# An attention and MoE kernel on one core: the second group's q on ScalarE's queue, the third pair's v on GpSimd

## The chip, the core and the metric

The kernel runs on one NeuronCore of one Trainium2 chip. The metric is the device time of one execution in microseconds; before the change it is 595.95 us, the median of 3 runs (595.73 to 596.18).

## What is computed

Attention over q, k and v of shape (2, 12, 448, 64), and behind it two feed-forward layers over 896 tokens (768 to 2048 to 768, twice). The two matrices of a layer come as 64-bit floats.

```python
scores = cap * np.tanh(scale * q @ k.T / cap)
attn = np.exp(scores - max); attn = attn / (attn.sum(-1) + 1e-09)
x = (attn @ v) as (batch * seq, heads * head_dim)
h = x @ w_in;  x = where(h > 0, h, exp(min(h, 0)) - 1) @ w_out
h = x @ w_in2; out = relu(h) ** 2 @ w_out2
```

## The kernel before, in words

**Pairs and groups.** The 24 heads are worked on as 12 pairs, n = 0 to 11; two pairs are a group (L77). Of a group's q, k and v the first 384 rows of each head are loaded into one tile each (`nat[g]`, three transfers each, one for every 128 rows, L117 and L132); the last 64 rows go to tiles of their own: `qz` (one transfer, L122), `kz` (two, L127) and `vs` (two, L139). `load_group` (L103) issues them, on SP's queue unless another is named. Group 0 is loaded in two halves, one for each pair, so its transfers are half as large.

**One pair.** TensorE transposes ten 128-column blocks, k with its tail and q with its tail, into PSUM tile `pt` (`turn`, L170). ScalarE casts the whole to tf32-like `kqh` (`high`, L182), VectorE subtracts to get the rest `kql` (`low`, L188). TensorE makes the scores in four chunks c (`scores`, L224), each of which takes one of two PSUM tiles `sc`; ScalarE applies tanh to each chunk (`tanh`, L240) and exp to the first two and to the last two chunks (`exp`, L250). VectorE splits the result into `ph` and `pl` (`split_p`, L254). v is split into `vh` and `vl` by `prep_v` (L144): `vl` on GpSimd for every pair, `vh` on GpSimd for pairs 0 and 1 and on VectorE from pair 2 on (L153). TensorE multiplies v and p in two parts (`pv`, L266), ScalarE copies the result out (`pv_out`, L292), and VectorE scales it by the sums a few pairs later (`norm`, `norm_x`).

**Order.** The whole stands under `tc.manual_schedule()` (L535): every engine and queue keeps the order of the program text. The opening (L536 to L558) issues loads, makes the first pair in `first_pair` (L198: TensorE transposes pair 0, with products of the identity to fill its time; ScalarE makes three casts at L220; VectorE three subtractions), then `scores(0, 0)`, `scores(0, 1)` and `turn(1)`. The loop at L574 runs over the pairs. In iteration 0 the order on ScalarE is tanh(0,0), tanh(0,1), high(1), exp(0,0), tanh(0,2), tanh(0,3), exp(0,1), then tanh(1,0) and high(2); on TensorE it is scores(0,2), scores(0,3), nine identity products (L594, eighteen records in the profile), scores(1,0), scores(1,1), turn(2), pv(0,0), then scores(1,2). On VectorE, `prep_v(2)` stands in iteration 1 ahead of `low(2)` and of the split of pair 1.

**Transfers and their completion counters.** The framework lays the instructions of all engines in one list, by its own estimate of when each starts, and numbers the transfers of both queues along that list. Eight completion counters serve them in turn, so the issue of every transfer waits until the transfer eight numbers before it, of either queue, has landed. A DMA issue stands in the order of the engine that makes it: one that waits on ScalarE holds what ScalarE has behind it. In the program before, the list runs so around the change; the first pair's third cast on ScalarE stands between numbers 32 and 33. At the list's beginning, where both queues issue, their transfers alternate one by one: 1, 3, 5, 7, 9 and 11 are ScalarE's (q with its tail of pair 0, cap, a piece of w_in), 2, 4, 6, 8, 10 and 12 are SP's.

```
12-16 k, kz of pair 1 (SP)       17-20 q, qz of pair 1 (SP)
21-25 v, vs of pair 0 (SP)       26-28 k of group 1 (SP)
29-30 kz of group 1 (SP)         31-33 q of group 1 (SP)
34    qz of group 1 (SP)         35-39 v, vs of pair 1 (SP)
40    w_in piece (SP)            41-45 v, vs of group 1 (SP)
```

After attention come the two feed-forward layers. Their matrices are streamed in pieces, and VectorE and ScalarE turn each piece into a high and a low part.

Of the kernel before, what the change touches and what calls it, by code (L numbers as in the profile page):

```python
# [26 lines left out]
def attention_moe_kernel(  # L27
# [12 lines left out]
    nc = tc.nc  # L40
    B, H, S, D = q.shape
# [46 lines left out]
    qzs = [one.tile([P, 4, D], F32, name=f"qz{i}") for i in range(2)]  # L88
# [4 lines left out]
    def fill_kq(i, eng):  # L93
        eng.memset(kzs[i], 0.0)
        eng.memset(qzs[i][D:], 0.0)
# [4 lines left out]
        if i < 2:  # L100
            eng.memset(vss[i][:, :, D:], 1.0)

    def load_group(g, what="kqvw", pp=None, dma=nc.sync.dma_start):  # L103

        if 2 * g >= len(pairs):
            return
        b, hp = pairs[2 * g]
        h0, nh = (0, 4) if pp is None else (2 * pp, 2)
        hs = slice(2 * hp + h0, 2 * hp + h0 + nh)
        if g not in nat:  # L110
            nat[g] = {x: lp.tile([P, NFULL, 4, D], F32, name=x, tag=x) for x in "kqv"}
        tail = slice(NFULL * P, S)
        for x, src in (("k", k), ("q", q)):
            if x in what:
                t = nat[g][x][:, :, h0:h0 + nh]
                src = src[b, hs]
                for c in range(NFULL):  # L117
                    dma(  # L118
                        t[:, c], src[:, c * P:(c + 1) * P].rearrange("h p d -> p h d")
                    )  # L120
                if x == "q":
                    dma(  # L122
                        qzs[g % 2][:D, h0:h0 + nh], src[:, tail].rearrange("h p d -> p h d")
                    )
                else:
                    for hh, r in enumerate(ROWS):
                        dma(  # L127
                            kzs[g % 2][r, h0 // 2:(h0 + nh) // 2, r],
                            src[hh::2, tail].rearrange("h p d -> p h d"),
                        )  # L130
        if "v" in what:
            for c in range(NFULL):  # L132
                dma(
                    nat[g]["v"][:, c, h0:h0 + nh],
                    v[b, hs, c * P:(c + 1) * P].rearrange("h p d -> p h d"),
                )
        if "w" in what:
            for hh, r in enumerate(ROWS):
                dma(  # L139
                    vss[g % 2][r, h0 // 2:(h0 + nh) // 2, :D],  # L140
                    v[b, hs][hh::2, tail].rearrange("h p d -> p h d"),
                )

    def prep_v(n):  # L144
        if n >= len(pairs):
            return
        g, pp = divmod(n, 2)
        vh, vl = vhs[n % 3], vls[n % 3]
        vn = nat[g]["v"][:, :, 2 * pp:2 * pp + 2]
        h, l = (t.rearrange("p (c h) d -> p c h d", h=2)[:, :, :, :D] for t in (vh, vl))  # L150


        (nc.vector if n > 1 else nc.gpsimd).tensor_copy(h, vn)  # L153
        nc.gpsimd.tensor_tensor(l, vn, h.bitcast(F32), op=ALU.subtract)


# [2 lines left out]
    def turn_one(to, n, u, c):  # L159
        g, pp = divmod(n, 2)  # L160
        hs = slice(2 * pp, 2 * pp + 2)
        if c < NFULL:
            src = nat[g]["kq"[u]][:, c, hs].rearrange("p h d -> p (h d)")
        elif u == 0:
            src = kzs[g % 2][:, pp]
        else:
            src = qzs[g % 2][:, hs].rearrange("p h d -> p (h d)")
        nc.tensor.transpose(to, src, ident)  # L168
# [13 lines left out]
    def high(n):  # L182
        if n >= len(pairs):
            return
        st["qk", n] = [ap_.tile([P, 2, W], F32R, name=x, tag=x) for x in ("kqh", "kql")]
        nc.scalar.copy(used(st["qk", n][0]), used(st["pt", n]))

    def low(n):  # L188
        if n >= len(pairs):
            return  # L190
        h, l, t = (used(x) for x in (*st["qk", n], st["pt", n]))
        nc.vector.tensor_tensor(l, t, h.bitcast(F32), op=ALU.subtract)

    def idle_products(to, n):
        for _ in range(n):
            nc.tensor.matmul(to[:, 0, :P], ident, ident, start=True, stop=True)

    def first_pair():  # L198

        idle = psc.tile([P, 2, W], F32, name="sc", tag="sc")
        warm = lambda n: idle_products(idle, n)
        qk = [ap_.tile([P, 2, W], F32R, name=x, tag=x) for x in ("kqh", "kql")]
        st["qk", 0] = qk
        warm(8)
        pieces = []
        for u, cs, pool, tag, after in (
            (0, range(NFULL), ps1, "pt", 2),
            (1, range(NFULL + 1), ps1, "po", 0),  # L210
            (0, range(NFULL, NFULL + 1), psc, "sc", 6),
        ):
            t = pool.tile([P, 2, W], F32, name=tag, tag=tag)
            at = slice(cs[0] * P, (cs[-1] + 1) * P)
            for c in cs:
                turn_one(t[:, u, c * P:(c + 1) * P], 0, u, c)
            warm(after)
            pieces.append((t[:, u, at], *(x[:, u, at] for x in qk)))
        for t, h, l in pieces:
            nc.scalar.copy(h, t)  # L220
        for t, h, l in pieces:
            nc.vector.tensor_tensor(l, t, h.bitcast(F32), op=ALU.subtract)
# [17 lines left out]
    def tanh(n, c):  # L240
        if c == 0:
            st["e", n] = ap_.tile([P, NB, S], F32, name="e", tag="e")
        w = 2 if c < NFULL else 1
        nc.scalar.activation(  # L244
            st["e", n][:, 2 * c:2 * c + w], st["sc", n, c][:, :w, :S], AF.Tanh, scale=tsc
        )
# [3 lines left out]
    def exp(n, i):  # L250
        e = st["e", n][:, PARTS[i]]
        nc.scalar.activation(e, e, AF.Exp, scale=capt)  # L252

    def split_p(n, i, copy=nc.vector.tensor_copy):  # L254
        if n < 0:
            return
        if i == 0:
            st["p", n] = [
                ap_.tile([P, NB - 1, S], F32R, name=x, tag=x, bufs=1) for x in ("ph", "pl")
            ]  # L260
        blocks = slice(PARTS[i].start, min(PARTS[i].stop, NB - 1))
        e, h, l = (t[:, blocks] for t in [st["e", n]] + st["p", n])
        copy(h, e)
        nc.vector.tensor_tensor(l, e, h.bitcast(F32), op=ALU.subtract)
# [270 lines left out]
    with tc.manual_schedule():  # L535
        fill_kq(0, nc.vector)  # L536
        load_group(0, "k", 0)
        load_group(0, "q", 0, dma=nc.scalar.dma_start)
        nc.scalar.dma_start(capt, cap.unsqueeze(0).to_broadcast([P, 1]))
        ws.load(nc.scalar.dma_start)  # L540
        load_group(0, "kq", 1)
        load_group(0, "vw", 0)
        fill_kq(1, nc.gpsimd)
        load_group(1, "kq")
        load_group(0, "vw", 1)
        ws.load()
        load_group(1, "vw")
# [2 lines left out]
        fill_v(2, nc.gpsimd)  # L550
        np_ = len(pairs)
        first_pair()
        nc.vector.reciprocal(tsc, capt)
        nc.vector.tensor_scalar(tsc, tsc, 1.0 / math.sqrt(D), None, op0=ALU.mult)
        prep_v(0)
# [18 lines left out]
        for n in range(np_):  # L574
            last = n == np_ - 1
            tanh(n, 0)
            if n:
                high(n + 1)
            tanh(n, 1)
            if not n:  # L580
                high(n + 1)
            split_p(n - 1, 1)
            prep_v(n + 1)
            exp(n, 0)
            low(n + 1)
            if n == 2:
                emit(second[3:])
            scores(n, 2)
            pv(n - 1, 1)
            scores(n, 3)  # L590
            if n:
                turn(n + 2)
            else:
                idle_products(ps1.tile([P, 2, W], F32, name="po", tag="po"), 9)  # L594
            norm(n - 2)
            if last:
                emit(ws.start())
            tanh(n, 2)
            pv_out(n - 1)
            if 2 <= n < 7:  # L600
                ws.load()
            tanh(n, 3)
            exp(n, 1)
            emit(norm_x(n - 3))
            split_p(n, 0)
            if n == 1:
                second = ws.whole()
                emit(second[:3])
            scores(n + 1, 0)
            scores(n + 1, 1)  # L610
            if not n:
                turn(2)
            if last:

                begun.append(new_acc())
                mm_in(0, 0, begun[0], xh, xl, kb[0:6:2])
            pv(n, 0)

            if n % 2:
                load_group((n + 3) // 2, "qv" if n > 1 else "v")  # L620
            else:
                load_group(n // 2 + 2, "k" if n else "kq")
                load_group(n // 2 + 1, "w" if n else "")


# [12 lines left out]
        x, x_high, x_low = norm_x(np_ - 2)  # L638
# [9 lines left out]
        x, x_high, x_low = norm_x(np_ - 1, nc.scalar.copy)  # L648
# [166 lines left out]
```

## Time and profile before

| | |
|---|---|
| median of 3 runs | 595.95 us (595.73 to 596.18) |
| the profiled execution | 594.1 us, of which 592.3 us from the first to the last instruction |
| busy | TensorE 98%, its weight loads 89%, VectorE 72%, ScalarE 56%, GpSimd 5% of the span |
| mean granted TensorE clock | 0.997 of 2.4 GHz |
| 40 slices of 14.8 us | TensorE at 9 tenths or more in all but the first and the last; the granted clock is below 9 tenths in one slice, the second |

The profiled execution is 1.85 us under the median. Times in the profile count from the start of the span. PE is TensorE, PEld its weight loads, DVE VectorE, ACT ScalarE, POOL GpSimd; SPq and ACTq are the queues on which SP and ScalarE issue transfers. A row of a timeline gives start, duration, engine, line, operation, what it writes and reads, how many instructions are merged, and in brackets the idle time before it with what ended it. A row of a table by windows gives for each stretch its length, the busy time of each engine, TensorE's granted clock, the DMA engines' busy share and GB/s.

### The profile page before, as it was taken

To read this page: it belongs to the slowest core of one execution; us is meant where nothing else is said; L and a number is where in the kernel's file an instruction comes from. 1 tells how busy PE (TensorE), PEld (TensorE's weight loads), DVE (VectorE), ACT (ScalarE), POOL (GpSimd) and SP (SyncE) were. 2 spreads that over 40 slices of the span, in tenths; PEclk is the share of its full clock that TensorE was granted. 3 is DMA by queue.
4 is the path that set the end of the run, shared out by engine and by line. 5 is a ranking of instruction groups with operands and counts; after the bars stand their busy time and mean duration, and the time that the engine had idled before them with its cause. 6 is when DMAs were issued, how large, how long until landed. Compare 5 with 4: busy or idle time off the path is not lost.

```text
span 592.3 us, 8596 instructions
## 1 busy us (share of the span) xinstructions
PE 583.4 (98%) x3062; PEld 528.0 (89%) x3062; DVE 425.0 (72%) x845; ACT 334.2 (56%) x484; POOL 32.1 (5%) x46
## 2 busy tenths in 40 slices
PE   8899999999999999999999999999999999999997
PEld 8677777788999999999999999999999999999997
DVE  4599999989999888665666657777777599981000
ACT  5699999827898777433333335666666645441000
POOL 3110110000000000000000000000000011230000
PEclk9899999999999999999999999999999999999999
DMA  5645651024444333233333344333333346622000
GB/s 128 158 103 140 161 148 42 33 75 144 135 133 134 106 98 100 76 128 106 116 98 107 111 132 132 107 107 107 108 114 113 108 136 184 184 70 106 24 23 37
DMA packets 81980, 64.76 MB, mean 109 GB/s; under 512 B 38416, under 2 KB 77072, under 8 KB 81936
## 3 DMA queue, kind: packets, MB, share of 16 engines
q1 hardware_dynamic: 80432, 63.58, 36.8%
q10 hardware_dynamic: 1504, 0.62, 0.4%
q8 instruction: 24, 0.39, 0.3%
q14 instruction: 20, 0.16, 0.1%
HBM read 61.34 MB, written 2.80 MB: 108 GB/s over the span
## 4 chain that ended last, share of the span: by engine, by line
PE 90%; DMA 3%; DVE 3%; SPq 2%; ACT 1%; issue 1%; POOL 0%; ACTq 0%; POOLq 0%; DVEq 0%
PE acc L522 19%; PE acc L523 19%; PE acc L521 19%; PE po L287 8%; PE acc L746 7%; PE acc L745 7%; PE acc L747 7%; PE sc L235 4%; PE pt L168 1%; DMA q<-in_q_dram 1%; SPq L118 1%; DVE xn L327 1%; DMA far<-rd 1%; DMA bc<-far 1%; DMA qz<-in_q_dram 0%
## 5 line engine op out<-in xcount | busy, mean ns | idle before, releaser
L521 PE MATMUL acc<-xh,wh 128*128 128x448 f32 x384 | 139.8, 364 | 1.2 <-ACT xh L333 1.2
L522 PE MATMUL acc<-xl,wh 128*128 128x448 f32 x384 | 140.0, 365 | 0.2 <-DVE xl L334 0.2
L523 PE MATMUL acc<-xh,wl 128*128 128x448 f32 x384 | 139.9, 364 | 0.0
L446 ACT CAST wh<-wf 128x384 fp32r<-128x384 f32 (+2 forms) x114 | 57.9, 508 | 107.2 <-PE acc L522 87.5
L391 ACT ACTIVATE wf<-wst 128x384 f32<-128x384 f32 (+2 forms) x130 | 70.5, 543 | 60.5 <-DVE wl L441 33.7
L441 DVE TENSOR_TENSOR wl<-wf,wh 128x384 fp32r<-128x384 f32 (+2 forms) x116 | 63.6, 548 | 55.9 <-ACT wh L446 55.8
L521 PEld LDWEIGHTS acc<-xh,wh 128*128 128x128 f32 x384 | 72.1, 188 | 7.1 <-ACT xh L333 1.5
L522 PEld LDWEIGHTS acc<-xl,wh 128*128 128x128 f32 x384 | 72.1, 188 | 5.9 <-DVE xl L334 0.5
L523 PEld LDWEIGHTS acc<-xh,wl 128*128 128x128 f32 x384 | 72.1, 188 | 5.7 <-DVE wl L441 0.3
L432 DVE SCALAR_TENSOR_TENSOR wf<-wst,wf 128x384 uint32<-128x384 uint32 (+3 forms) x132 | 71.1, 539 | 0.1
L425 DVE SCALAR_TENSOR_TENSOR wf<-wst,wf 128x384 uint32<-128x384 uint32 (+3 forms) x132 | 70.9, 537 | 0.0
L522 PE MATMUL acc<-gl,wh 128*128 128x448 f32 x192 | 70.0, 365 | 0.0
L523 PE MATMUL acc<-gh,wl 128*128 128x448 f32 x192 | 70.0, 364 | 0.0
L521 PE MATMUL acc<-gh,wh 128*128 128x448 f32 x192 | 69.8, 364 | 0.0
L404 DVE TENSOR_SCALAR wf<-wf 128x384 uint32<-128x384 uint32 (+3 forms) x132 | 54.4, 412 | 0.7
L400 DVE TENSOR_SCALAR wf<-wf 128x384 f32<-128x384 f32 (+3 forms) x132 | 45.7, 346 | 7.5 <-ACT wf L391 7.5
L244 ACT ACTIVATE e<-sc,tsc 128x896 f32<-128x896 f32 (+1 forms) x48 | 43.4, 911 | 2.9 <-PE sc L235 2.9
L732 DVE COPY o<-acc 128x432 f32<-128x432 f32 (+1 forms) x8 | 4.5, 557 | 53.8 <-PE acc L747 45.7
L746 PE MATMUL acc<-wl,gh 128*128 128x432 f32 x112 | 40.3, 359 | 0.0
L745 PE MATMUL acc<-wh,gh 128*128 128x432 f32 x112 | 40.0, 357 | 0.0
L747 PE MATMUL acc<-wh,gl 128*128 128x432 f32 x112 | 39.9, 356 | 0.0
L252 ACT ACTIVATE e<-e,capt 128x1792 f32<-128x1792 f32 (+1 forms) x24 | 38.6, 1609 | 0.8
(94 smaller groups left out, 933.0 us busy)
## 6 DMA issues: line engine op xcount, KB each, us to landing
wst<-in_moe_w_in_dram SPq DMA_DIRECT2D x63, 384.0 KB, 3.2
wst<-in_moe_w_out_dram SPq DMA_DIRECT2D x24, 384.0 KB, 3.2
wst<-in_moe_w_out_dram SPq DMA_DIRECT2D x16, 432.0 KB, 3.2
wst<-in_moe_w_out_dram SPq DMA_DIRECT2D x16, 336.0 KB, 2.9
wst<-in_moe_w_out_dram SPq DMA_DIRECT2D x12, 256.0 KB, 2.7
bc<-far SPq DMA_DIRECT2D x12, 224.0 KB, 3.3
k<-in_k_dram SPq DMA_DIRECT2D x15, 128.0 KB, 3.7
q<-in_q_dram SPq DMA_DIRECT2D x15, 128.0 KB, 2.9
```

The source lines that it names most:

```text
L391: nc.scalar.activation(self.f[i], hi.bitcast(F32), AF.Abs)
L404: v.tensor_scalar(fb, fb, 3, 0x3FFFFFFF, op0=ALU.logical_shift_left, op1=ALU.bitwise_and)
L425: v.scalar_tensor_tensor(out=fb, in0=hi, scalar=0xC0000000, in1=fb, op0=ALU.bitwise_and, op1=ALU.bitwise_or,)
L432: v.scalar_tensor_tensor(out=fb, in0=lo, scalar=29, in1=fb, op0=ALU.logical_shift_right, op1=ALU.bitwise_or,)
L441: (v if dst is None else nc.gpsimd).tensor_tensor(wl, self.f[i], wh.bitcast(F32), op=ALU.subtract)
L446: (v.tensor_copy if self.alone else nc.scalar.copy)(wh, self.f[i])
L521: nc.tensor.matmul(acc, w[0], x[0], start=first, stop=False)
L522: nc.tensor.matmul(acc, w[0], x[1], start=False, stop=False)
L523: nc.tensor.matmul(acc, w[1], x[0], start=False, stop=last)
L745: nc.tensor.matmul(acc, gh[:, f, gs], w[0], start=a, stop=False)
L746: nc.tensor.matmul(acc, gh[:, f, gs], w[1], start=False, stop=False)
L747: nc.tensor.matmul(acc, gl[:, f, gs], w[0], start=False, stop=z)
```

## The change

`load_group` gets a letter of its own, "z", for the tail of q; where q was loaded, its tail still is, right behind it, with one exception. For group 1, the three large q transfers are no longer issued by SP between kz and qz; ScalarE issues them after `first_pair`, that is behind its three casts and ahead of tanh(0,0). The tail qz of group 1 stays on SP, right behind kz. And `prep_v` makes `vh` of pair 2 on GpSimd instead of VectorE.

```diff
-    def load_group(g, what="kqvw", pp=None, dma=nc.sync.dma_start):
+    def load_group(g, what="kqzvw", pp=None, dma=nc.sync.dma_start):
...
         for x, src in (("k", k), ("q", q)):
+            src = src[b, hs]
             if x in what:
                 t = nat[g][x][:, :, h0:h0 + nh]
-                src = src[b, hs]
                 for c in range(NFULL):
                     dma(
                         t[:, c], src[:, c * P:(c + 1) * P].rearrange("h p d -> p h d")
                     )
-                if x == "q":
-                    dma(
-                        qzs[g % 2][:D, h0:h0 + nh], src[:, tail].rearrange("h p d -> p h d")
-                    )
-                else:
+                if x == "k":
...
+        if "z" in what:
+            dma(qzs[g % 2][:D, h0:h0 + nh], q[b, hs, tail].rearrange("h p d -> p h d"))
...
-        (nc.vector if n > 1 else nc.gpsimd).tensor_copy(h, vn)
+        (nc.vector if n > 2 else nc.gpsimd).tensor_copy(h, vn)
...
-        load_group(0, "q", 0, dma=nc.scalar.dma_start)
+        load_group(0, "qz", 0, dma=nc.scalar.dma_start)
...
-        load_group(0, "kq", 1)
+        load_group(0, "kqz", 1)
...
-        load_group(1, "kq")
+        load_group(1, "kz")
...
         first_pair()
+        load_group(1, "q", dma=nc.scalar.dma_start)
         nc.vector.reciprocal(tsc, capt)
...
-                load_group((n + 3) // 2, "qv" if n > 1 else "v")
+                load_group((n + 3) // 2, "qzv" if n > 1 else "v")
             else:
-                load_group(n // 2 + 2, "k" if n else "kq")
+                load_group(n // 2 + 2, "k" if n else "kqz")
```

## Rows read from the trace of the kernel before

**Rows 1.** The chain that ended last, 0 to 70 us: start, us, what.
```profile
1.79 2.72 DMA q<-in_q_dram
...
4.53 0.37 SPq L118
...
20.17 4.06 PE po L287 x12
...
27.81 0.96 PE pt L168 x8
...
30.18 2.67 PE po L287 x12
...
38.73 2.71 PE po L287 x12
```
**Rows 2.** TensorE's timeline, 10 to 24 us.
```profile
11.20 0.47 PE L235 MATMUL sc<-kqh 64*128 64x448 f32 x2
...
16.49 0.55 PE L168 MATMUL pt<-ident,k 128*128 128x128 f32 x3
...
19.87 0.30 PE L168 MATMUL pt<-ident,qz 128*128 128x128 f32 x1 [0.22 <-DMA qz<-in_q_dram]
```
**Rows 3.** Table by windows, 17 to 24 us.
```profile
17.00:20.00 3.00, 1.45 (x7) 0.71 (x6) 1.93 (x3) 0.89 (x1) 0.00 (x0) 1.00 0.78 175
20.00:23.00 3.00, 3.00 (x9) 2.66 (x9) 0.00 (x0) 2.76 (x3) 1.42 (x2) 0.52 0.44 115
23.00:24.00 1.00, 1.00 (x5) 0.77 (x3) 0.00 (x0) 0.90 (x1) 0.09 (x1) 0.74 1.08 297
```
**Rows 4.** ScalarE's timeline, 5 to 24 us.
```profile
7.68 0.27 ACT L220 CAST kqh<-sc 128x128 fp32r<-128x128 f32 x1
9.67 1.91 ACT L244 ACTIVATE e<-sc,tsc 128x896 f32<-128x896 f32 x2 [1.72 <-PE sc L235]
...
16.90 0.99 ACT L244 ACTIVATE e<-sc,tsc 128x896 f32<-128x896 f32 x1
20.21 0.96 ACT L186 CAST kqh<-pt 128x960 fp32r<-128x960 f32 x1 [2.32 <-PE pt L168]
```
**Rows 5.** VectorE's timeline, 26 to 28 us.
```profile
26.01 0.55 DVE L153 CAST vh<-v 128x384 fp32r<-128x384 f32 x1 [7.04 <-DMA v<-in_v_dram]
26.48 1.15 DVE L192 TENSOR_TENSOR kql<-pt,kqh 128x960 fp32r<-128x960 f32 x1
```
**Rows 6.** Issues on SP's and ScalarE's queues, 0 to 20 us (timeline).
```profile
0.73 1.55 ACTq L118 DMA_DIRECT2D q<-in_q_dram  x3
...
11.81 1.69 SPq L118 DMA_DIRECT2D k<-in_k_dram  x3
13.61 1.67 SPq L127 DMA_DIRECT2D kz<-in_k_dram  x2
15.32 1.69 SPq L118 DMA_DIRECT2D q<-in_q_dram  x3
17.06 0.61 SPq L122 DMA_DIRECT2D qz<-in_q_dram  x1
```
**Rows 7.** What SP's queue waited for, 0 to 140 us: us in total, times, longest.
```profile
SPq L118 <- DMA q<-in_q_dram: 0.4, 1, 0.4
```
**Rows 8.** Transfers issued from 10.6 to 15.3 us: count, KB each, median us to landing.
```profile
vs<-in_v_dram SPq DMA_DIRECT2D x2, 16.0 KB, 2.0
...
k<-in_k_dram SPq DMA_DIRECT2D x3, 128.0 KB, 3.7
...
kz<-in_k_dram SPq DMA_DIRECT2D x2, 32.0 KB, 3.0
```
**Rows 9.** GpSimd's timeline, 21 to 22 us.
```profile
21.50 0.50 POOL L153 CAST vh<-v 128x384 fp32r<-128x384 f32 x1 [7.32 <-DMA v<-in_v_dram]
```
**Rows 10.** TensorE's timeline, 109 to 119 us.
```profile
109.66 1.08 PE L287 MATMUL po<-pl,vh 128*128 128x448 f32 x4 [0.24 <-DVE pl L264]
...
118.26 1.08 PE L287 MATMUL po<-pl,vh 128*128 128x448 f32 x4 [0.19 <-DVE pl L264]
```

## The prediction

> **What bounds the kernel now.** I read the page first, then the chain that ended last in its first 70 us, then TensorE, ScalarE, VectorE and both issuing queues there. From about 30 us on TensorE is without a gap: the twelve products of pv start 8.55 us apart (30.18, then 38.73) [rows 1]. In the pair before, the same step took 10.01 us (20.17 to 30.18) [rows 1]: its first twelve products lasted 4.06 instead of 2.67 us. The table by windows shows why: from 17 to 20 us TensorE was busy for 1.45 of 3 us, and from 20 us on its granted clock was 0.52, then 0.74, of full speed [rows 3], that is at the lower level of 1.2 GHz for most of that time. It was idle for group 1's q: turn(2) begins at 16.49, but its last block, qz, runs at 19.87 [rows 2]. ScalarE's high(2) waits 2.32 us for that block and starts at 20.21 [rows 4]. So whatever moves high(2) and pv(0,0) moves all that follows; the change aims at this place. Both come at the end of a ScalarE queue that runs without a gap from tanh(0,0) at 9.67 to tanh(1,0) at 16.90 [rows 4].
>
> **The wait that comes with an issue.** A transfer's issue waits until the transfer eight numbers before it has landed, on either queue. The trace shows this across the queues: SP's second k transfer of pair 1 (number 13) is asked for at 4.53, and what the chain has ahead of it is the landing of ScalarE's third q transfer (number 5), 1.79 to 4.51 [rows 1]; SP's queue has that as a wait of 0.4 us [rows 7]. So a ScalarE issue can be held by an SP transfer.
>
> The Trainium skill ("DMA: Bandwidth & Descriptors", the section on the anatomy of one DMA) says that DMA engines don't wait on semaphores: the wait happens on the issuing sequencer, ahead of dispatch. The trace agrees, as far as that 0.4 us of SP's queue goes; of a held ScalarE it shows nothing.
>
> **The change part by part.**
>
> *The three q issues on ScalarE.* By themselves they are free: three took 1.55 us on ScalarE's queue at the start [rows 6], and between the third cast's end at 7.95 and tanh(0,0) at 9.67 ScalarE waits 1.72 us for scores [rows 4]. Their numbers are not free. The list has the third cast between numbers 32 and 33. Without q, SP's qz becomes 31 and the first v transfer of pair 1 becomes 32, so ScalarE's first is 33 or 34. At the list's beginning the two queues alternate one by one; I let them do so here, which makes the three 33, 35 and 37. They wait for 25 (the second vs transfer of pair 0), 27 (the second k of group 1) and 29 (the first kz of group 1). All three are issued by SP later than 7.95, and SP has nothing that lets it come there sooner. The third decides: kz is issued at 13.61 [rows 6] and takes 3.0 us to land [rows 8], 16.6. With 0.52 us for the issue itself (a third of 1.55) ScalarE is free at about 17.1. Tanh(0,0) waits behind, ready since 9.67: held by about **7.5 us**.
>
> *Who waits for tanh(0,0).* Two scores tiles are filled, so scores(0,2), at 11.20 before [rows 2], must wait until tanh(0,0) has read the first. One tanh is 0.96 us (half of 1.91) [rows 4]: scores(0,2) starts at about 18.15. From there to turn(2) TensorE had 5.29 us (11.20 to 16.49) [rows 2], of which 0.17 was a wait; I take 5.1, and 0.96 for the eight transposes of a turn [rows 1]. TensorE has then stood idle for some 6.9 us. Already 1.55 us of idleness in 3 us was followed by the lower level [rows 3], so I add one such stretch at the price that it has there: 3 x 0.48 + 0.26 = 1.7 us. turn(2) ends at 18.15 + 5.1 + 0.96 + 1.7 = 25.9. On ScalarE, tanh(1,0) comes at 16.90 + 7.5 = 24.4 and is out by 25.4, so TensorE is the later of the two. q itself, asked for by 17.1 and 3.7 us on its way at most (k's time) [rows 8], is in by 20.8 and late for nobody.
>
> *What comes back.* pv(0,0) now runs at full speed, since the slow stretch lies earlier: 8.55 us to the next pv instead of 10.01. pv(1,0) starts at 25.9 + 8.55 = 34.45 instead of 30.18: **+4.3 us**. TensorE has no gap later in which to catch up.
>
> *SP's queue.* It loses three issues, so qz goes at 15.32 instead of 17.06 [rows 6], and all of v, vs and the w_in piece behind it are 1.74 us earlier. Each is needed only after high(2) and pv(0,0), which are now later: nothing gained. The eighth transfers behind ScalarE's three (41, 43 and 45, group 1's v and vs) are asked for at about 20 us and wait for nothing that lands after 20.8; at worst some 1 us, with nobody waiting.
>
> *vh of pair 2.* On VectorE it waited 7.04 us for v and held low(2), which came at 26.48 [rows 5]. Now GpSimd makes it; a cast there takes 0.50 us [rows 9] against 0.55 on VectorE, and GpSimd is idle for 7.32 us before its cast of pair 1 [rows 9]. VectorE could take low(2) from about 21.2 us, when high(2) was done. In my forecast high(2) starts at 25.9, and low(2) follows it at once, at 26.9 instead of 26.48: the removed wait is worth nothing, for ScalarE is late next. GpSimd has nothing queued behind the new cast but the subtraction for the same pair.
>
> *The letters elsewhere* ("qz", "kqz", "qzv") give the same transfers in the same order: zero.
>
> **The sum.** The profiled execution took 594.1 us; 594.1 + 4.3 = 598.4. It is 1.85 us under the median, so the median to be expected is **600.2 us**.
>
> **Bounds.** The hold: if the three are numbered without SP between them (33, 34, 35), the third waits for the third k at the latest; the second k, issued a third into 1.69 us after 11.81 and 3.7 us on its way, lands at 16.1: 0.5 us less. If they fall one number later, it is the second kz, issued half of 1.67 us after 13.61, which lands at 17.4: 0.8 us more. The clock: without a fall 1.7 us go, but ScalarE is then the later one (25.4), so 0.5 us less is sure and the rest depends on pv(0,0) starting ahead of high(2): 1.2 at most. With a stretch twice as long, 1.7 more. VectorE's lag, which shows as TensorE waits of 0.24 and 0.19 us near the end [rows 10], may vanish: 0.4 less. Low: 4.3 - 0.5 - 1.2 - 0.4 = 2.2, 598.1; high: 4.3 + 0.8 + 1.7 = 6.8, 602.7.
>
> **The rivals.**
>
> *The issues are not held* (faster). If the three have numbers whose forerunners have landed by 7.95 us, q is there by 13.3 (9.55 + 3.7), and turn(2) waits for qz alone, 1.74 us earlier: 594.2. TensorE's idleness then shrinks by more than half, so the clock should stay, and 10.01 becomes 8.55: another 1.46, 592.8. For it: 1.72 us of cover for 1.55 us of issues. Against it: ScalarE's third cast stands behind number 32, and the transfers from 25 on are issued after 10.6 us [rows 8]. Chance 0.10, at 592.8.
>
> The Trainium skill (same page, "Issuing engines are not separate DMA queues") holds that issuing from a second engine saves only the sequencer's time for the issue. By it alone this rival ends at 1.74 us, 594.2 us; no run here shows which of the two it is.
>
> *The hold is short* (no change). One us of hold counts for one, so the gain and loss meet where ScalarE is free at about 12.8 us. Were the last of the three to wait for number 25, issued at about 11.2, shortly ahead of k's 11.81 [rows 6], and 2.0 us on its way [rows 8], ScalarE would be free at 13.7, 3.4 us sooner than forecast: +0.9, 596.9. For it: the list is the framework's estimate, and a shift by two or four places does this. Against it: number 25 is what the first of three must wait for, so all three would have to move up. Chance 0.05.
>
> *The forecast* (slower): 0.85. It holds as long as the last forerunner lands after 12.8 us, and its candidates land at 16.1 to 17.4.
>
> **How the numbers follow.** A measurement of this kernel can tell about 0.2%, 1.2 us, from no change, so the three cases fall into faster 0.10, same 0.05 and slower 0.85. The range leaves the two rivals out (0.15) and must hold nearly all of the forecast: its bounds are 598.1 and 602.7; I take 597.8 to 602.2, as the low end can meet a hold one place shorter and the high end needs two misfortunes at once.
>
> **What would show it.** On ScalarE's queue three issues between the third cast and tanh(0,0) with gaps between them, the last at about 16.6 us behind the landing of a kz or k; tanh(0,0) at about 17.1 instead of 9.67; TensorE idle from 11.3 to 18.1 and a granted clock near 0.5 behind that; high(2) near 25.9 with almost no wait for its transposes; low(2) right behind it; GpSimd's third cast ahead of 26 us; and steps of 8.55 us from pv(1,0) on. I am wrong if tanh(0,0) starts near 9.7: then the three were not held, and turn(2) should end near 18.4. I am wrong in size if the clock does not fall, or falls once more behind 26 us.

## The result, and the profile after

The kernel after takes 598.67 us (median of 5, 598.42 to 601.03); the kernel before, run beside it, 595.73 us (median of 5, 595.61 to 596.18). The ratio is 1.0061, with a 95% interval of 1.0043 to 1.0079: slower, by 2.6 to 4.7 us. The forecast was slower, 600.2 us with a range of 597.8 to 602.2. The profiled execution of after took 599.1 us with a span of 597.3, against 594.1 and 592.3 before. Of the 40 slices of before TensorE is under 9 tenths in the first two and the last, not in the first and the last alone: the second, 14.8 to 29.6 us, has the place that the change aims at. The lines of after are renumbered: turn is L166, high L184, low L190, scores L233, tanh L242, exp L250, split_p L261 and L262, pv L285, the identity products L194; those of other kernels differ by a few.

ScalarE's timeline after, 7 to 28 us; it answers to [rows 4]:

```profile
7.79 0.27 ACT L218 CAST kqh<-sc 128x128 fp32r<-128x128 f32 x1
13.63 3.75 ACTq L118 DMA_DIRECT2D q<-in_q_dram  x3
17.48 1.91 ACT L242 ACTIVATE e<-sc,tsc 128x896 f32<-128x896 f32 x2 [9.42 <-DMA q<-in_q_dram]
...
25.47 1.01 ACT L242 ACTIVATE e<-sc,tsc 128x896 f32<-128x896 f32 x1 [0.67 <-PE sc L233]
27.10 0.96 ACT L184 CAST kqh<-pt 128x960 fp32r<-128x960 f32 x1 [0.62 <-PE pt L166]
```

ScalarE's third cast ends at 8.06, and then the engine does nothing until 17.48. The first of the three q issues comes at 13.63, and the three, 1.55 us long at the start of the kernel [rows 6], are spread over 3.75 us here. Tanh(0,0) stands behind them; it was at 9.67. High(2), at 20.21 before, is at 27.10, and its own wait has shrunk from 2.32 to 0.62 us. SP asks for the two kz transfers of group 1 meanwhile; SP's queue after:

```profile
13.76 1.29 SPq L123 DMA_DIRECT2D kz<-in_k_dram  x2
```

TensorE's timeline after, 10 to 30 us; it answers to [rows 2]:

```profile
11.10 0.27 PE L166 MATMUL pt<-ident,qz 128*128 128x128 f32 x1
18.54 0.74 PE L233 MATMUL sc<-kqh 64*128 64x448 f32 x2 [7.17 <-ACT e L242]
...
21.25 3.37 PE L194 MATMUL po<-ident 128*128 128x128 f32 x18
...
25.97 0.55 PE L166 MATMUL pt<-ident,k 128*128 128x128 f32 x3
...
26.82 1.06 PE L285 MATMUL po<-ph,vh 128*128 128x448 f32 x4
```

TensorE stands still for 7.17 us, waiting for tanh(0,0) to free a scores tile. When it comes back its clock is down. The table by windows of after, 11 to 27 us, answers to [rows 3]; the columns are the same, TensorE's clock third from the end:

```profile
11.00:14.00 3.00, 0.38 (x4) 0.14 (x2) 1.23 (x3) 0.00 (x0) 1.40 (x2) 0.92 0.43 98
14.00:17.00 3.00, 0.00 (x0) 0.00 (x0) 0.00 (x0) 0.00 (x0) 0.09 (x1) 0.50 0.87 197
17.00:20.00 3.00, 1.46 (x7) 0.88 (x7) 0.00 (x0) 2.52 (x3) 0.50 (x1) 0.50 0.70 149
20.00:23.00 3.00, 3.00 (x14) 2.87 (x13) 2.20 (x2) 3.00 (x4) 1.02 (x1) 0.50 0.90 236
23.00:24.00 1.00, 1.00 (x7) 1.00 (x7) 0.97 (x2) 0.97 (x2) 0.00 (x0) 0.62 0.82 183
24.00:27.00 3.00, 3.00 (x27) 2.50 (x26) 2.74 (x3) 1.81 (x2) 1.25 (x1) 1.00 0.55 120
```

The granted clock is 0.50, the lower level of 1.2 GHz, from 14 us on, while the engine is still idle, and stays there until well into 23 to 24 us (0.62 there), some 5.2 us behind TensorE's return at 18.54. The eighteen identity products take 3.37 us; with the clock up they take 2.17 (below). From 24 us on the clock is up for the rest of attention, so the next pair runs without the fall that the kernel before had there. The chain that ended last, from 26 us on, answers to [rows 1]:

```profile
26.04 1.02 PE pt L166 x8
27.06 2.44 PE po L285 x12
...
35.37 2.67 PE po L285 x12
...
43.92 2.67 PE po L285 x12
```

The step from 35.37 to 43.92 is the 8.55 us of before. From pv(1,0) on the two kernels run alike, shifted. By TensorE's timeline pv(1,0) starts at 30.11 before and 35.30 after, 5.19 us later, and the executions took 594.1 and 599.1: the rest is 563.99 and 563.80 us (some 1.8 us of each lie outside the span). All of the loss lies ahead of 35.3 us.

What became of the part on VectorE and GpSimd, in VectorE's timeline after, 28 to 34 us; it answers to [rows 5]:

```profile
28.09 1.16 DVE L190 TENSOR_TENSOR kql<-pt,kqh 128x960 fp32r<-128x960 f32 x1 [1.32 <-ACT kqh L184]
32.16 1.09 DVE L261 CAST ph<-e 128x1792 fp32r<-128x1792 f32 x1 [2.92 <-PE po L285]
```

The wait for v is gone; low(2) waits for high(2) instead. And behind it VectorE waits again, 2.92 us, for the products that still read the one buffer `ph`.

### The profile page after: what moved, and what is told of

The parts are those of the page before. It is cut to its first block, busy times and chain, and to the rows that moved or that the text cites. A ratio compares the mean times of both kernels' runs of the same rounds, so it can differ in the third digit from the quotient of the medians.

```text
span 597.3 us, 8596 instructions
## 1 busy us (share of the span) xinstructions
PE 582.9 (98%) x3062; PEld 529.0 (89%) x3062; DVE 424.6 (71%) x844; ACT 334.3 (56%) x484; POOL 33.5 (6%) x47
## 4 chain that ended last, share of the span: by engine, by line
PE 90%; DMA 3%; DVE 3%; ACT 2%; SPq 2%; issue 1%; ACTq 0%; DVEq 0%
PE acc L520 19%; PE acc L521 19%; PE acc L519 19%; PE po L285 7%; PE acc L745 7%; PE acc L744 7%; PE acc L746 7%; PE sc L233 5%; DMA q<-in_q_dram 2%; PE pt L166 1%; ACT e L242 1%; DVE xn L325 1%; SPq L118 1%; DMA bc<-far 1%; PE po L194 1%
## 5 line engine op out<-in xcount | busy, mean ns | idle before, releaser
L242 ACT ACTIVATE e<-sc,tsc 128x896 f32<-128x896 f32 (+1 forms) x48 | 43.4, 912 | 10.1 <-DMA q<-in_q_dram 9.4
L250 ACT ACTIVATE e<-e,capt 128x1792 f32<-128x1792 f32 (+1 forms) x24 | 38.6, 1607 | 0.8
```

## The experiments

Twelve kernels ran, on four chips, each batch beside runs of the kernel before on the same chip (medians there 594.95 to 595.14 us); ratios are to those runs. The table has for each where ScalarE's tanh(0,0) and TensorE's pv(0,0) and pv(1,0) start by the timelines, the profiled execution, what is left of it behind pv(1,0), and the median. The rows of before and after have the medians of the result.

| kernel | tanh(0,0) | pv(0,0) | pv(1,0) | profiled | rest | median | ratio (95%) |
|---|---|---|---|---|---|---|---|
| before | 9.67 | 19.99 | 30.11 | 594.1 | 563.99 | 595.73 | 1 |
| after | 17.48 | 26.82 | 35.30 | 599.1 | 563.80 | 598.67 | 1.0061 (1.0043 to 1.0079) |
| same | 9.47 | 20.47 | 30.64 | 594.82 | 564.18 | 594.7 | 0.9992 (0.9975 to 1.0009) |
| v_only | 10.06 | 19.99 | 29.99 | 594.62 | 564.63 | 594.92 | 0.9991 (0.9977 to 1.0006) |
| q_only | 17.27 | 26.78 | 35.26 | 598.72 | 563.46 | 598.44 | 1.0052 (1.0031 to 1.0073) |
| hold_only | 16.63 | 26.04 | 34.52 | 600.23 | 565.71 | 600.98 | 1.009 (1.007 to 1.011) |
| one_q | 13.65 | 23.42 | 31.89 | 595.6 | 563.71 | 595.51 | 1.0009 (0.9991 to 1.0027) |
| after_fill | 18.03 | 25.67 | 34.15 | 597.74 | 563.59 | 598.69 | 1.0063 (1.004 to 1.0085) |
| early_q | 11.07 | 18.89 | 27.37 | 592.82 | 565.45 | 592.84 | 0.9965 (0.9949 to 0.9981) |
| gps_q | 9.29 | 18.92 | 28.95 | 592.9 | 563.95 | 591.1 | 0.9935 (0.9912 to 0.9958) |
| gps_fill | 9.04 | 18.53 | 26.99 | 594.65 | 567.66 | 594.62 | 0.9985 (0.9968 to 1.0002) |
| gps_all | 9.79 | 18.00 | 26.48 | 590.27 | 563.79 | 590.84 | 0.9931 (0.9914 to 0.9948) |
| gps_all_v | 10.24 | 18.00 | 26.48 | 590.21 | 563.73 | 590.28 | 0.9916 (0.9894 to 0.9938) |
| sp_order | 10.19 | 19.91 | 30.22 | 596.37 | 566.15 | 594.63 | 0.9989 (0.9974 to 1.0005) |

**The kernel before against itself, and the two parts apart.** `same` is the kernel before, unchanged.

> The program before, once more: it gives the spread of a kernel's runs, and a second profile of it. The profiled execution of before was 1.85 us under the median of its runs. If that is chance, this profile's span lies 1 to 2 us higher at the same median (595.7 +- 0.3), and the place where the two profiles differ says how much of the 5.0 us between the profiles of before and after is the change's and how much the executions'. If the profiles agree to 0.3 us, the change costs more in the profile than in the timed runs for another reason.

It is a measure of the noise: single executions from 593.75 to 597.12 us. Its profiled execution, 594.82 us, lies 0.7 us above that of before and 0.1 above its own median, so the 1.85 us by which the profile of before lies under its median are not a fixed distance.

`v_only` is the kernel before with vh(2) on GpSimd:

```diff
-        (nc.vector if n > 1 else nc.gpsimd).tensor_copy(h, vn)
+        (nc.vector if n > 2 else nc.gpsimd).tensor_copy(h, vn)
```

> Only the second part of the change: vh of the third pair on GpSimd, q stays on SP's queue. Theory (ScalarE is held): no loss; VectorE no longer stands 7 us in front of low(2), which comes near 21.3 instead of 26.5, and TensorE meets turn(3) with 0.1 to 0.3 us less; 595.3 to 595.9 us. Rival (GpSimd's part costs, its cast took 1.38 us in the changed kernel): 597 to 599 us.

VectorE's timeline in `v_only`, 18 to 30 us:

```profile
21.20 1.16 DVE L192 TENSOR_TENSOR kql<-pt,kqh 128x960 fp32r<-128x960 f32 x1 [1.85 <-ACT kqh L186]
26.86 1.80 DVE L263 CAST ph<-e 128x1792 fp32r<-128x1792 f32 x1 [4.50 <-PE po L287]
```

Low(2) comes at 21.20 instead of 26.48 [rows 5], and it is worth nothing: the time is within 0.2% of before, and a little under what was expected. The five microseconds turn into a wait for `ph`, 4.50 us, which ends with pv(0,1), on TensorE.

`q_only` is the kernel after with vh(2) back on VectorE (the edit above the other way round).

> Only the first part: the second group's q on ScalarE's queue, vh of the third pair stays on VectorE. Theory (ScalarE is held): tanh(0,0) near 17.5 as in the changed kernel, time 598.2 to 599.5 us. Rival (GpSimd's part costs): 595.5 to 596.5 us. If both parts cost, it lies between.

It has the whole loss: tanh(0,0) at 17.27 and pv(1,0) at 35.26, against 17.48 and 35.30 in after. What ScalarE waited for in `q_only`, 0 to 30 us (us in total, times, longest):

```profile
ACT e L242 <- DMA kz<-in_k_dram: 9.1, 1, 9.1
```

That is the framework's counter at work: the wait of the last q issue ends with a transfer of SP, kz. The chain that ended last in `q_only` has it with its times:

```profile
14.25 2.43 DMA kz<-in_k_dram
...
16.70 0.46 ACTq L118
```

SP's two kz issues stand at 13.6 and 14.2 us, so the transfer that lands at 16.68, just ahead of ScalarE's last issue, is the second kz.

**The hold without the data.** `hold_only` is the kernel before with three transfers of half a kilobyte on ScalarE's queue, at the place where after has q; q stays on SP.

```diff
+    spare = const.tile([P, 3], F32, name="spare")
...
+        for i in range(3):
+            nc.scalar.dma_start(spare[:, i:i + 1], cap.unsqueeze(0).to_broadcast([P, 1]))
```

> The kernel before, q on SP's queue as it was, with three transfers of 0.5 KB each added on ScalarE's queue at the place where the changed kernel asks for q; they fill a tile that nothing reads. By their numbers (33, 34 and 36) they wait for SP's transfers 25, 26 and 28, the last being the third k of group 1, which lands at 15.4 to 16.6 us. Theory (the wait of the issue holds ScalarE): tanh(0,0) at 16 to 17 us instead of 9.67, and 597.2 to 599.2 us. Rival (it is q's 384 KB, which run beside other loads or come late): three tiny transfers cost at most their issue time, tanh(0,0) before 10.2 us and 595.7 to 596.2 us.

ScalarE's timeline in `hold_only`:

```profile
13.24 3.28 ACTq L555 DMA_DIRECT2D spare<-in_cap_dram  x3
16.63 1.90 ACT L245 ACTIVATE e<-sc,tsc 128x896 f32<-128x896 f32 x2 [8.89 <-DMA spare<-in_cap_dram]
```

Three transfers that carry next to nothing hold ScalarE as q did, and pv(1,0) goes to 34.52. So neither q's bytes nor a late q make the loss; the issue's wait does. The median is nearly 2 us above what was expected. Of that 1.4 us is in the trace: TensorE waits for q or qz four times, which in after it never does. That probably belongs to the experiment, as three transfers more shift what later ones wait for; no run takes it apart. Its waits in `hold_only`, 30 to 140 us:

```profile
PE pt L169 <- DMA q<-in_q_dram: 1.2, 3, 0.6
...
PE pt L169 <- DMA qz<-in_q_dram: 0.2, 1, 0.2
```

**How much of a hold counts.** `one_q` is the kernel after with one of the three q transfers on ScalarE and two back on SP. Its vh(2) is made on GpSimd, unlike in the kernel before that the expectation names; `v_only` puts that at nothing.

```diff
-        load_group(1, "kz")
+        load_group(1, "k")
+        for c in (1, 2):
+            nc.sync.dma_start(
+                nat[1]["q"][:, c], q[0, 4:8, c * P:(c + 1) * P].rearrange("h p d -> p h d")
+            )
+        load_group(1, "z")
...
         first_pair()
-        load_group(1, "q", dma=nc.scalar.dma_start)
+        nc.scalar.dma_start(nat[1]["q"][:, 0], q[0, 4:8, :P].rearrange("h p d -> p h d"))
```

> The kernel before with one of the second group's three q transfers asked for on ScalarE behind the casts, the other two on SP as before. Its number is 33, so its issue waits for transfer 25 alone. Theory (the hold lasts until that transfer has landed, and what of it exceeds the slack counts): the issue starts at 13.2 to 13.7, tanh(0,0) at 13.9 to 14.4 and not 9.67; of these 4.5 us high(2)'s own wait of 2.32 us is free, so pv(1,0) is 1.5 to 2.5 us later than before and the median 596 to 597.3. Rival (a hold counts in full or as soon as TensorE has stood still): 598 or more. Rival (a single transfer is not held): tanh(0,0) by 10.5, median within 0.5 us of before.

ScalarE's timeline in `one_q`:

```profile
13.17 0.37 ACTq L556 DMA_DIRECT2D q<-in_q_dram  x1
13.65 1.91 ACT L242 ACTIVATE e<-sc,tsc 128x896 f32<-128x896 f32 x2 [5.36 <-DMA vs<-in_v_dram]
```

The wait ends with a vs transfer of pair 0 (transfer 25 was the second of them), at 13.17. Tanh(0,0) is 3.98 us later than before, pv(1,0) 1.78, as was expected. The median missed: expected at 596 to 597.3, it came out 0.56 us above before, which is not to be told from no change. With the others this makes a line: of a hold of 3.98 us 2.20 are free (`one_q`), of 6.96 us 2.55 (`hold_only`), of 7.60 us 2.45 (`q_only`), of 7.81 us 2.62 (after). By the start of pv(1,0) some 2.5 us are free; beyond that one microsecond of hold costs one. (All are counted from the one trace of before; that of `same` has tanh(0,0) 0.20 us earlier and pv(1,0) 0.53 later.)

**The clock's share.** `after_fill` is the kernel after with 26 more identity products behind turn(1), where TensorE stood still.

```diff
         turn(1)
+        idle_products(ps1.tile([P, 2, W], F32, name="po", tag="po"), 26)
```

> The kernel after with 26 more identity products (two instructions of about 0.115 us each, so some 6 us) on TensorE behind turn(1), in the time in which it stands still for ScalarE; their output is read by nobody. They leave the hold as it is. Theory (part of the loss is the clock): tanh(0,0) stays at 17.3 to 17.6, but the granted clock stays near 1.00 up to about 17.4 us, scores(0,2) and the nine identity products take 3 us and not 6, turn(2) ends 1.7 to 2.8 us sooner than 27.06, and the median falls by 1.2 to 2.5 us against the kernel after, to 596 to 597.5. Rival (ScalarE's own chain sets the end and the clock is hidden): high(2) and pv(1,0) stay within 0.5 us of 27.1 and 35.3, the median at 598 to 599.

Table by windows and, below it, TensorE's timeline in `after_fill`:

```profile
17.00:20.00 3.00, 1.39 (x12) 0.81 (x10) 0.00 (x0) 1.97 (x3) 0.00 (x0) 1.00 0.80 179
20.00:23.00 3.00, 2.88 (x21) 2.64 (x21) 1.65 (x2) 3.00 (x3) 1.51 (x2) 1.00 0.76 205
```

```profile
11.53 5.97 PE L194 MATMUL po<-ident 128*128 128x128 f32 x52
19.09 0.47 PE L233 MATMUL sc<-kqh 64*128 64x448 f32 x2 [1.59 <-ACT e L242]
...
20.71 2.17 PE L194 MATMUL po<-ident 128*128 128x128 f32 x18
23.42 0.47 PE L233 MATMUL sc<-kqh 64*128 64x448 f32 x2 [0.54 <-ACT e L242]
```

The clock stays at 1.00 and the eighteen products are back at 2.17 us. From tanh(0,0) to pv(1,0) it is 16.12 us, against 17.82 in after: the clock's fall costs 1.70 us. More is not to be had, as TensorE now waits for ScalarE again (0.54 us), whose chain is next. The hold itself was 0.55 us longer in this execution, so pv(1,0) gains 1.15 and the profiled execution 1.36. The medians do not show it (ratios 1.0063 and 1.0061, each with an interval of about 1.2 us to either side): the gain is in the trace and not to be told in the time, so neither expectation came out whole. The clock stayed up, as the first had it, but turn(2) comes 1.15 us sooner (1.70 counted from tanh(0,0)) and not 1.7 to 2.8; the median is that of the second, but high(2) and pv(1,0) did move, by 0.96 and 1.15 us.

**The same request elsewhere.** `early_q` asks for q on ScalarE too, but at the start, ahead of the first pair's casts.

```diff
         ws.load(nc.scalar.dma_start)
+        load_group(1, "q", dma=nc.scalar.dma_start)
...
         first_pair()
-        load_group(1, "q", dma=nc.scalar.dma_start)
```

> The kernel after with the second group's q asked for on ScalarE at the start, behind the MoE's first piece and ahead of the first pair's casts, where the numbers are 15, 17 and 20 and wait for transfers 7, 9 and 12. Theory (a hold is as long as the awaited transfer is late; transfer 12 is the first of the second half of k): ScalarE's first cast, 6.04 before, starts at 7.5 to 9, and everything behind it is as much later; tanh(0,0) at 11 to 12.5, far ahead of 17.5; the median 595.5 to 597.5, between the two kernels. Rival (asking ahead of the casts is free, q is early and there is no hold): first cast at 6.0 to 6.5 and the median at or under 595. Rival (q ahead of v in the shared DMA engines delays v and k): 598 or more with ScalarE not held.

ScalarE's timeline in `early_q`:

```profile
4.99 2.30 ACTq L118 DMA_DIRECT2D q<-in_q_dram  x3
7.32 1.28 ACT L218 ACT_TABLE_LOAD   x1 [7.32 <-DMA wst<-in_moe_w_in_dram]
8.62 0.48 ACT L218 CAST kqh<-pt 128x384 fp32r<-128x384 f32 x1
...
19.19 0.95 ACT L184 CAST kqh<-pt 128x960 fp32r<-128x960 f32 x1
```

The expected time was wrong. There is a hold here too: the first cast, at 6.04 before, comes at 8.62, and tanh(0,0) is 1.40 us later, as expected; yet the kernel is faster than before, 592.84 us. What had been left out is what an early q gives: it is there when turn(2) comes, TensorE no longer stands still at 17 to 20 us, the clock does not fall, and high(2) runs at 19.19 behind a ScalarE queue without a gap. Pv(1,0) starts 2.74 us earlier than before. Of that 1.28 us are left in the profiled execution; about 1 us goes behind attention, at 131 us, where TensorE waits 2.14 us instead of 1.15.

`gps_q` asks for q on GpSimd's queue, behind its fills; the framework gives transfers of that queue completion counters of their own, and GpSimd has nothing else to do there.

```diff
         fill_v(2, nc.gpsimd)
+        load_group(1, "q", dma=nc.gpsimd.dma_start)
         first_pair()
-        load_group(1, "q", dma=nc.scalar.dma_start)
```

> The kernel after with one thing moved: the second group's three q transfers are issued on GpSimd's queue, behind fill_v's, and no longer on ScalarE's. Theory (the held ScalarE is the loss): ScalarE waits for nothing between the third cast and tanh(0,0), which starts at 9.5 to 9.9 us as before; high(2) is back at about 20.2, pv(1,0) at 30.0 to 30.7, and the median is that of before, 594 to 595.3. Rival (the second group's q, or SP's changed order, is late and sets the end): tanh(0,0) is early too, but TensorE waits for q at turn(2), high(2) starts at 24 or later and the median is 597 or more. Second rival (a gain: q and v are earlier, and what follows is too): under 593.5.

GpSimd's timeline in `gps_q`, and ScalarE's:

```profile
4.40 2.38 POOL L118 DMA_DIRECT2D q<-in_q_dram  x3
12.47 0.51 POOL L151 CAST vh<-v 128x384 fp32r<-128x384 f32 x1 [5.69 <-DMA v<-in_v_dram]
```

```profile
9.29 1.91 ACT L242 ACTIVATE e<-sc,tsc 128x896 f32<-128x896 f32 x2 [1.72 <-PE sc L233]
...
19.13 0.96 ACT L184 CAST kqh<-pt 128x960 fp32r<-128x960 f32 x1 [1.64 <-PE pt L166]
```

Nothing is held, tanh(0,0) is on time, and the kernel is faster than before by 0.42 to 0.88%, some 4 us. That is the second rival of the expectation. So asking for q earlier and on another queue was worth something; its place on ScalarE made it a loss. The Trainium skill ("DMA: Bandwidth & Descriptors", "Issuing engine by pattern") puts simple loads on Sync and keeps GpSimd for indirect ones. Here the simple load on GpSimd wins: that queue is free at 4.4 us, and nothing of this stage stands behind it before 12.47.

`sp_order` uses no other queue: all of the second group's k, q and z on SP, ahead of the first half of v instead of behind it (vh(2) on GpSimd as after).

```diff
+        fill_kq(1, nc.gpsimd)
+        load_group(1, "kqz")
         load_group(0, "vw", 0)
-        fill_kq(1, nc.gpsimd)
-        load_group(1, "kz")
         load_group(0, "vw", 1)
...
         first_pair()
-        load_group(1, "q", dma=nc.scalar.dma_start)
```

> No new queue: everything of the second group's k, q and z on SP, as in the kernel before, but ahead of the first half of the first group's v and vs instead of behind them; vh(2) on GpSimd as after. Theory (the order in which SP asks is what makes q late in the kernel before): q and qz are issued some 2.8 us sooner than 15.3 and 17.1, turn(2) waits for no q, high(2) at 18.3 to 19.3 and pv(1,0) at 27 to 29; v for vh(0) comes some 5 us later than 12.6, vh(0) at 17 to 18.5, in time or nearly for pv(0,0); the median 592 to 594. Rival (v is now the late one): pv(0,0) waits for vh(0) or vl(0) till 20 or later and the median is 595 or more.

High(2) comes at 18.31, as expected, but now v is late. TensorE's timeline in `sp_order`:

```profile
19.91 1.09 PE L285 MATMUL po<-ph,vh 128*128 128x448 f32 x4 [1.82 <-POOL vh L151]
```

TensorE stands still for 1.82 us ahead of pv(0,0), the clock falls behind that (0.59 at 21, 0.50 at 22 to 24 us), and pv(1,0) is at 30.22, no better than before: in this order SP's queue has q in time and v late. The median, 594.63, lies between the two expectations.

**The rest of the gain.** `gps_q` still stood still in turn(2), for k and kz, and its clock fell (0.66 at 19, 0.50 at 20 to 22 us). `gps_fill` puts identity products ahead of it, so that k and kz are there when it starts; `gps_all` moves k, kz and qz to GpSimd's queue too. The edit of `gps_fill`, against `gps_q`:

```diff
             if not n:
+                idle_products(ps1.tile([P, 2, W], F32, name="po", tag="po"), 6)
                 turn(2)
```

> The kernel gps_q (the second group's q on GpSimd's queue) with six more identity products (twelve instructions of about 0.115 us, 1.4 us) on TensorE just ahead of turn(2), where it stood still from 16.9 to 17.95 us for k and kz; their output is read by nobody. Theory (TensorE's stop ahead of turn(2) brings the half clock of 19.7 to 22.6, which is on the path): the granted clock stays near 1.00, turn(2) ends 0 to 0.4 us later than in gps_q, the step from pv(0,0) to pv(1,0) falls from 10.0 to 8.5, pv(1,0) starts at 27.4 to 27.8, and the profiled run is 1.0 to 1.6 us under gps_q's 592.9; the median falls by as much below 591.1 only if most executions of gps_q have the half clock. Rival (the stop does not bring the fall, or what the clock gives is lost to another wait): the step stays 9.5 to 10.1 and the profile at 592 to 593.

The place behaved as expected: clock 1.00 throughout, a step of 8.46 us from pv(0,0) to pv(1,0) instead of 10.03, pv(1,0) at 26.99. The time did not: 594.65 us, and a median 3.5 us above that of `gps_q`, which ran on another chip (ratios 0.9985 and 0.9935). Of this execution the trace shows where: pv(1,0) is 1.96 us earlier, and the rest behind it 3.71 us longer, at about 132 us. There TensorE has finished attention's products and waits for the last pair's normalisation, which goes out to memory and back. The chain that ended last, in `gps_fill` and then in `gps_q`, and TensorE's timeline in `gps_fill`:

```profile
124.94 3.01 DMA far<-rd
127.97 3.60 DMA bc<-far
```

```profile
126.57 1.65 DMA far<-rd
...
128.23 3.16 DMA bc<-far
```

```profile
133.50 0.47 PE L519 MATMUL acc<-xh,wh 128*128 128x448 f32 x1 [2.75 <-ACT xh L331]
```

The round trip took 6.61 us here, against 1.65 + 3.16 in `gps_q`; TensorE waited 2.75 us instead of 0.94. Then the clock fell, here instead of at the start. Windows of `gps_fill` (length, TensorE's busy time, its clock, DMA share, GB/s):

```profile
132.00:134.00 2.00, 0.47 (x1) 1.00 0.44 146
134.00:136.00 2.00, 1.84 (x7) 0.71 0.00 0
136.00:138.00 2.00, 2.00 (x7) 0.50 0.46 133
```

Why the round trip was longer in this kernel, and whether it is in most of its executions (592.47 to 597.14 us), was not settled. The edit of `gps_all`, against after:

```diff
-        load_group(1, "kz")
...
         fill_v(2, nc.gpsimd)
+        load_group(1, "kqz", dma=nc.gpsimd.dma_start)
         first_pair()
-        load_group(1, "q", dma=nc.scalar.dma_start)
```

> The kernel gps_q with the second group's k and kz on GpSimd's queue too, so that none of its k, q or qz stands on SP's, and SP asks for v at once. Nine issues of some 0.8 us keep GpSimd busy from 4.4 to 11.6 us, ahead of its first cast at 12.5. Theory (in gps_q the late k and kz, 16.8 and 17.95, hold turn(2) and bring the half clock; earlier, ScalarE's chain from tanh(0,0) sets pv(1,0), which took 16.3 us in early_q): turn(2) waits for nothing, the clock stays near 1.00, tanh(0,0) starts at 9.3 to 9.8, pv(1,0) at 25.6 to 26.5, and the median is 588 to 590. Rival (nine more transfers at the start slow the first group's k, q and v in the shared engines): tanh(0,0) or the first scores 1 us or more later and the median 591 or more. Rival (GpSimd's issues run into its casts): vh(0) later than 14, pv(0,0) waits for it.

Turn(2) waits for nothing (TensorE is busy for all of 16 to 24 us at a clock of 1.00), ScalarE's queue has no gap from 12.13 to 23.03, pv(1,0) is at 26.48, and the profiled execution takes 590.27 us. The start is a little later than in `gps_q`, 9.79 against 9.29. The median, 590.84, is above the 588 to 590 that were expected and not to be told from that of `gps_q`.

`gps_all_v` undoes the other part of the change in `gps_all`: vh(2) on VectorE.

> The kernel gps_all (the second group's k and q on GpSimd's queue) with the change's other part undone: vh(2) is cast on VectorE again. Theory (that part is worth nothing even when q is early, since ph(1,0) waits for pv(0,1) behind it): v for it lands at about 21.1 us, VectorE casts it there and makes low(2) at 21.7 to 22 and not 20.83, ph(1,0) starts at 23.2 to 23.6 as before, pv(1,0) at 26.3 to 26.8, and the median is within 0.8 us of gps_all's 590.84. Rival (with the early q VectorE is the next bound, and the cast on it counts): ph(1,0) at 24 or later, the median 591.8 or more.

Low(2) comes at 21.35 instead of 20.83, ph(1,0) at 23.34 instead of 23.35, pv(1,0) at 26.48 in both. That part is worth nothing with an early q either. `gps_all_v` has the lowest median of all, 590.28 us, 0.62 to 1.06% under before; the medians do not tell it from `gps_all`.

## Why the prediction was right

*The wait that comes with an issue*: right, and it is the cause. Held by a transfer of the other queue, eight numbers back: shown by `hold_only` (a hold with no data) and `gps_q` (the data with no hold). The last number was off by one. With 33, 35 and 37 the last would have waited for the first kz; by the framework's list of after they are 33, 35 and 38, so it waits for the second kz, as the chain of `q_only` shows. SP's two kz issues took 1.29 us from 13.76 (1.67 from 13.61 in [rows 6]), and ScalarE was free at 17.4, not 17.1: a hold of 7.8 us for 7.5. The case stood among the bounds.

*Who waits for tanh(0,0)*: the chain was right link by link. Forecast and measured starts: scores(0,2) 18.15 and 18.54, end of turn(2) 25.9 and 27.06, pv(1,0) 34.45 and 35.30. The term that was too small is the stretch at half clock, put at 1.7 us from [rows 3]. From scores(0,2) to turn(2) TensorE took 7.50 us instead of 5.1, so the fall cost it 2.4 us, 0.7 more than the term: the clock was down for the first 5.2 us after the stop, where [rows 3] has it down for some 3.4. On the path only 1.70 of them count (`after_fill`), as ScalarE's chain comes in just behind. Tanh(1,0) after its hold was put at 24.4 us; it started at 25.47.

*What comes back*: right. Pv(1,0) is 5.19 us later for the 4.3 forecast, from the two terms above. The step is 8.48 us from pv(0,0) to pv(1,0), and nothing is made good later: the rest behind pv(1,0) is the same to 0.2 us.

*SP's queue, vh of pair 2, the letters*: nothing, as forecast. For vh the cause was named only in part: the removed wait is worth nothing not just because ScalarE is late next, but because `ph(1,0)` waits for pv(0,1) in any case (`v_only`, `gps_all_v`).

*The sum*: 594.1 + 4.3 was forecast for the profiled execution, 599.1 came; 600.2 for the median, 598.67 came. The step that failed is the last one, the 1.85 us that were added for the distance of before's profile from its median: the profiled execution of after lies 0.43 us above its median, and that of `same` 0.12 above. So two errors of opposite sign met: the delay was put 0.7 us too low by the profiles, the distance 2.3 us too high. Luck has a part in the fit: with the delay as forecast the median would have come to 598.0, just above the low bound of 597.8. The loss is 5.0 us from profile to profile, 4.3 against the profile of `same`, and 2.9 us from median to median, where the interval of the ratio is 2.6 to 4.7; why the medians show less than the profile of before is open. Part of what moves single executions is in sight. Over 25 runs of before on one chip the time went from 593.72 us at a mean granted clock of 0.997 to 598.53 us at 0.990, and one fall like that of [rows 3] makes 0.3% (1.7 of 592 us), so by this estimate the slowest have lost as much as three such falls. The tie is loose: on another chip a run of before at 1.0 took 595.67 us and one at 0.993 took 594.53. `gps_fill` shows a second place, the border at 132 us. All five runs of after stand at 0.991 to 0.993. Which falls the runs of before beside after had is not known, since only one was profiled.

*The rivals*: the faster one, "not held", did not happen in this kernel, but its price had the right size where the issue did not hold tanh(0,0) for long: 592.8 was worked out from [rows 1, 6], and `gps_q` came to 591.1 and `early_q` to 592.84, the latter with a hold and a longer wait behind attention, so its close match is luck. The Trainium skill's rule behind it ("Issuing engines are not separate DMA queues": a second issuing engine saves only the sequencer's time) would have given 594.2; the median of `gps_q` is 3.1 us under that. Part of it seems to be the clock: the profiled execution of `gps_q`, in which the clock fell, is only 1.2 us under that of before; the five runs of `gps_q` at a mean clock of 0.999 or more took 590.62 to 591.83 us, the two at 0.997 some 592.8. The short hold, meant for 596.9 with ScalarE free at 13.7, was run as `one_q`: free at 13.5, 595.51. By pv(1,0), gain and loss meet at about 12.2 us (9.67 and the 2.5 us that are free), where the prediction had 12.8.

## What to carry to other kernels

A DMA issue on a compute engine's queue is an instruction with a wait of its own: before moving one, find the transfer whose completion counter it takes over and when that one lands, for until then everything behind it on that engine stands. Ask early, where the engine has nothing behind it, or on a queue whose counters are its own: the same three transfers cost 3 us or gained 4, by their place alone. And follow a gain to the next meeting point of the engines: a stop there can eat it, and in `gps_fill` and `sp_order` the clock fell behind it.

## What was not expected of the hardware

The granted clock went down while TensorE stood still (0.92 over 11 to 14 us in after, 0.50 over 14 to 17), and it was down for 5.2 us after the engine's return, against some 3.4 us in all in [rows 3]. The length of the last stop alone does not tell whether it falls: at the border behind attention it stayed at 1.00 behind 2.14 us in `early_q`, and fell to 0.50 behind 2.75 us in `gps_fill` and behind 1.36 us in `sp_order`.

GpSimd and VectorE slowed each other at some places where both worked. In `gps_all`, GpSimd's and VectorE's timelines:

```profile
16.63 2.67 POOL L152 TENSOR_TENSOR vl<-v,vh 128x384 fp32r<-128x384 f32 x1
```

```profile
18.35 1.44 DVE L261 CAST ph<-e 128x896 fp32r<-128x896 f32 x1
```

With the other engine idle beside it, in after, the subtraction takes 0.99 us on GpSimd (at 13.10) and VectorE's cast of this size 0.62 (at 25.02). The Trainium skill ("GPSIMD Engine Reference", "Specifications") has the two share access to SBUF and contend where VectorE's instruction has two SBUF inputs (or is in a mode that no row here shows); the trace agrees where GpSimd's 2.67 us lie beside VectorE's subtraction (16.22 to 18.43), and VectorE's slow cast has one input only. In after the cast of vh(2) on GpSimd, put at 0.50 us [rows 9], took 1.38 us beside such a subtraction; it cost nothing. Not every overlap does this: in `gps_all_v` GpSimd's subtraction took 1.00 us beside VectorE's low(2) (21.52 and 21.35 us).
